# Attention and gated MLP on one core: two more steps of score tiles, six more changes of V's bank, joins of maxima moved by a step, and an uneven split of the last output tile

## The chip, the core and the metric

The kernel runs on one core of one Trainium2 chip. The metric is the device time of one execution in microseconds (us). A core has five engines that run side by side, each working through its own instructions in order: TensorE (PE, matmuls; PEld is its weight load), VectorE (DVE), ScalarE (ACT), GpSimd (POOL) and SyncE (SP), which here only issues DMAs. They wait for each other through semaphores. An engine whose next instruction waits does nothing else in the meantime, and that holds for the DMAs that an engine issues too.

## What is computed

The reference, cut to what matters (S = 2048 rows, D = 512, 32 heads of 16, MLP width 1376):

```python
def _A_ref(x, wqkv, wo):
    qkv = ...                                  # x @ wqkv, split into heads
    scores = jnp.einsum("bhqd,bhkd->bhqk", q, k) * (Dh ** -0.5)
    p = _softmax(scores, axis=-1)
    o = jnp.einsum("bhqk,bhkd->bhqd", p, v)
    return o.transpose(...).reshape(B, S, D) @ wo
def _B_ref(x, w1, b1, w2, b2):
    return gelu(x @ w1 + b1) @ w2 + b2
xn = _layernorm(x)
out = x + _A_ref(xn, wqkv, wo) * _silu(_B_ref(xn, w1, b1, w2, b2))
```

## The kernel before

The first part (to about 437 us) does the layer norm, the projections and the MLP, whose result goes to DRAM (`g_d`). All of the change lies in the second part, the attention with the output projection.

**Units and steps.** Heads are taken in 8 groups of 4, queries in 4 chunks of 512: 32 *units* (`u`) of 16 *steps* each, steps `n` = 0 to 512. A step handles 128 keys of one unit. Every step writes four tiles of transposed scores (*T*, `t_one`, L760, banks `ps`, `two`, `pst` of the matmul memory), which ScalarE turns into exponentials (L763, L765), and it multiplies the exponentials of the step before by the values (*V*, `pv_step`, L832), into one bank for each unit. After step 16 of a unit, VectorE copies that bank out (L839).

**Maxima.** The exponentials need the row maxima of the scores beforehand. So the scores are computed once more, not transposed, one to two units ahead (*S*, `s_op`, L212), and VectorE reduces each tile to maxima (L218), two heads by two halves at a time. 588 of the 2048 tiles are done in the first part; `due(n)` says how many are to be done by step n: three a step, and two in the second step of the units 1 to `FEW`. The scores end at step `DONE` - 1 = 492. When a unit has all its maxima, VectorE *joins* them (`s_end0`, L274), transposes them (`s_turn`, L263), POOL splits them in two (L265, L266: tile `mh`), and after two to three more V the maxima are *sent* to DRAM (`s_send`, L296). From there SP loads them as two more rows of the query tile `qt` (`load_mh`, L182), which the first T of the unit needs. For the last unit, 31, two of the four writes of the maxima are issued by POOL.

**Banks.** S uses a ring of banks, in turn. In the units 1 to `FEW` = 16, V takes another bank than in the unit before (lines in `pv_step`: V's old bank goes into the ring, a bank of the ring becomes V's). From unit 17 on V keeps its bank, so the first V of a unit waits until VectorE has copied the unit before out of it; the first step of these units has another order (`FIRST`).

**Order within a step.** `manual_schedule` keeps the instructions in the order of the code. A string gives it: T, S, X and Y (two halves of a score tile), V, and from `DONE` on *H* and W. The entries of `todo[n, i]` come behind the T tile with number i of step n; pos=3 is behind the fourth.

**Output.** From `DONE` on there are no scores. H (`w_halves`) is a twelfth to an eighth part of two output tiles: 6 matmuls, in pairs, on the halves of the rows; the operands `oh`, `ol` are made two steps earlier by ScalarE (L938) and POOL (L941) in `w_two`. A pair of the 10 first output tiles takes 8 H in four steps. `gate` (ScalarE tanh L894, VectorE L895) prepares the gate of each token tile, `w_gate` (L966) multiplies the projection by it, `w_add` (L971) adds x, and a DMA (L972) writes it. V is done for two steps at once in every second step. The last output tile (t = 15) is split in two halves of 256 columns.

**Other work in these steps.** The sums of exponentials are inverted (`o_den`, L859 RECIPROCAL) in step 16u + 25, that is in the step with `ka` = 9 of the next unit; POOL divides by them (`o_div`, L871) in step 16u + 31.

Of the kernel before, what the change touches and what calls it, by code (L numbers as in the profile page):

```python
# [16 lines left out]
P = 128  # L17
S = 2048
D = 512
H = 32  # L20
DH = 16
KT = D // P
NT = S // P
# [11 lines left out]
NW = 10  # L35
EARLY = 4
AHEAD = ((-3, 0), (-3, 3), (-2, 0), (-2, 3))
DONE = 493
FILL0 = 2
APART = 5  # L40
HB = 5
# [2 lines left out]
ORDER = {0: "TTTTV", 2: "TSTTSTV", 3: "XTSTTYSTV"}  # L44
FIRST = "STXTTSYTV"
TWO = ("HTTTTHWV", "TTTTHHV")
BOTH = {DONE: "HHTTTTV", DONE + 3: "HHTTTTWV"}
SOON = 588
FEW = 16
SIDES = ((1, 1), (0, 0), (0, 1), (1, 0))  # L50
HC = CH // 2
PAIRED = 26
KB = 3
VP = (((0, 8),), ((0, 2), (1, 2)), ((2, 3),))
VB = (((0, 2), (1, 2)), ((1, 8),))
XB = 6
BANKS = ("ttvt", "xtmt", "ttvt")


@with_exitstack  # L60
def fused(ctx: ExitStack, tc: tile.TileContext, x, wqk, wv, wo, w1, b1, w2, out):
    nc = tc.nc
# [32 lines left out]
    def zip2(cols):  # L95
        return cols.rearrange("p (a b) -> p b a", a=2)

    def unzip(cols):
        return cols.rearrange("p (b a) -> p a b", a=2)

    def halves(cols):
        return cols.rearrange("p (a b) -> p a b", a=2)
# [12 lines left out]
    NU = NG * NCH  # L115
# [71 lines left out]
    later, ended, errands, sent = [], [], [], set()  # L187

    def units_of(u):
        return (u,) if u >= PAIRED else (u - u % 2, u - u % 2 + 1)  # L190

    def tick():
        for e in later:
            e[0] -= 1

    def flush():
        while later and later[0][0] <= 0:
            u = later.pop(0)[1]
            s_send(u)
# [36 lines left out]
    def s_op(op):  # L236
        if op == "S":
            if whole:
                s_whole(whole.pop(), 1)
            else:  # L240
                whole.append(jobs.pop(0))
                s_whole(whole[0], 0)
        elif op == "X":
            if not cut:
                cut[:] = [jobs.pop(0), 0]
            ps, pool = s_tile(True)
            x = s_mm(ps, cut[0], 0, 0, cut[1] * HC, HC)
            cut[2:] = [ps, pool, x]
        else:
            job, n, ps, pool, x = cut  # L250
            hold = nc.tensor.nop().ins
            tc.add_manual_dep(hold, x.name, SYNC, reason="row tile done")
            s_mm(ps, job, 1, HC, n * HC, HC)
            s_max(ps, job, slice(0, 2), n)
            s_ring.append(pool)
            cut[1] += 1
            if n:
                cut.clear()

    def s_turn(u, nm):  # L260
        later.append([8 if u == NU - 1 else 12, u])
        nt = qring.tile([P, 2 * GH * NCH], F32, name="nt", bufs=1)
        nc.vector.transpose(nt, nm)  # L263
        mh = MH[u] = qring.tile([P, 2, 2 * GH * NCH], F32R, name="mh", bufs=1)
        nc.gpsimd.tensor_copy(mh[:, 0], nt)  # L265
        nc.gpsimd.tensor_sub(mh[:, 1], nt, mh[:, 0].bitcast(F32))  # L266

    def s_end0(u):
        ended.remove(u)
        us = units_of(u)  # L270
        w = u % 2 * GH * NCH
        nm = nms[u // 2 % 2]
        mx = MX.pop(u).rearrange("p a b c n -> p (a b) (c n)")
        nc.vector.tensor_reduce(nm[:, w:w + GH * NCH], mx, axis=AX.X, op=OP.max, negate=True)  # L274
        if u == us[-1]:
            if "seen" in prog or u == NU - 1:
                s_turn(us[0], nm)
            else:
                put_off.append((us[0], nm))
        del QS[u]  # L280
        if "seen" in prog:
            ask_qs(u + 2)
        else:
            load_qs(u + 2)
# [127 lines left out]
    with ExitStack() as s1:  # L412
# [13 lines left out]
        def load_x(t, eng=nc.sync):  # L426
            xs[t] = w1k.tile([P, D], F32, name="xt", bufs=XB)
            eng.dma_start(xs[t], x[t * P:(t + 1) * P, :])
# [20 lines left out]
        def norm(t):  # L449
            xns[t] = w1k.tile([P, D], F32, name="xn", bufs=4)  # L450
            nc.vector.tensor_scalar(xns[t], xs.pop(t), mv[:, t, 0:1], ve[:, 4, t:t + 1],
                                    op0=OP.subtract, op1=OP.mult)
            if t + XB < NT:
                load_x(t + XB)

# [50 lines left out]
        for k in range(KT):  # L506
            nc.sync.dma_start(wv_r[:, k], wv[:, k])
        for t in range(6, XB):
            load_x(t)
# [209 lines left out]
    def quad(n, at):  # L719
        us = first[n]  # L720
        for u, b in zip(us, BANKS[n]) if at == 0 else ():
            if b == "t":
# [99 lines left out]
    def pv_step(u, k):  # L822
        g = u // NCH
        if k == 0:
            if 0 < u <= FEW:
                s_ring.insert(1, v_home.pop())
# [88 lines left out]
        w_round([(t, k) for t in T3], ot[NCH - 1][:, k].rearrange("p (t s) -> p t s", s=P), lo)  # L915

    def cols(t):
        n = 2 if t == NT - 1 else 1
        return [slice(i * D // n, (i + 1) * D // n) for i in range(n)]

    def w_mul(t, ks, parts=(0, 1)):
        if t not in PW:
# [41 lines left out]
    def w_gate(t, i=0):  # L964
        gx, cs = GX[t], cols(t)[i]
        nc.vector.scalar_tensor_tensor(gx[:, 0, cs], PW[t][i][:, :cs.stop - cs.start], 0.5, gx[:, 0, cs],  # L966
                                       op0=OP.mult, op1=OP.mult)

    def w_add(t, eng, i=0):
        gx, cs = GX[t], cols(t)[i]  # L970
        eng.tensor_add(gx[:, 0, cs], gx[:, 0, cs], gx[:, 1, cs])  # L971
        (nc.gpsimd if t < NW else nc.sync).dma_start(out[t * P:(t + 1) * P, cs], gx[:, 0, cs])  # L972

    def w_out(t, eng):
        w_gate(t)
# [2 lines left out]
    todo = {}  # L978

    def at(n, f, *a, pos=3):  # L980
        todo.setdefault((n, pos), []).append((f, a))
# [4 lines left out]
    def due(n):  # L986
        return min(4 * L, SOON + 3 * n - min(FEW, max(0, n - 1) // 16))

    for u in range(NU):
        g, c = divmod(u, NCH)  # L990
        if c == 0 and g == KB:
            for i in range(6):
                at(52 + i // 2, load_k, g, (i,), nc.gpsimd, 0, CH)
                at(56 + i // 2, load_k, g, (i,), nc.gpsimd, CH, CH)
                at(64 + i // 2, load_k, g, (i,), nc.gpsimd, S // 2, S // 2)
        elif c == 0 and g > KB:
            for i in range(6):
                at(64 * (g - KB + 1) + 6 + i, load_k, g, (i,), nc.gpsimd)
        if u >= 2:
            at(16 * u - 14, load_qt, u)  # L1000
            last = units_of(u)[-1]
            need = min(n for n in range(L) if due(n) >= 64 * (last + 1))
            need += 10 if u < PAIRED else 6 if u < NU - 1 else 2
            at(max(16 * u - 14, need), load_mh, u)
        if u < NU - 1:
            at(16 * u + 17, o_move, u, pos=0)
            at(16 * u + (25 if u < NU - 2 else 19), o_den, u, pos=0)
            at(16 * u + (27 if u < NU - 2 else 20), o_dn, u)
            at(16 * u + (31 if u < NU - 2 else 23), o_div, u, nc.gpsimd)
    T3 = range(NT - NCH, NT)  # L1010
    late = range(NW, NT)
    for t in range(NW):
        n = DONE + 4 * (t // 2)
        at(n - 3 + t % 2, load_gx, t)
        if t % 2 == 0:
            for i in range(2):
                at(n + i - 2 if t else n + 2 * i - 7, w_two, t, 2 * i)
            for i in range(4):
                for j in range(2):
                    at(n + i, w_halves, t, i % 2 * 2 + j, i // 2, pos="H")  # L1020
        at(n + t % 2, gate, t)
        at(n + 3, w_out, t, nc.gpsimd, pos="W")
    for i, t in enumerate(late):
        n = L - 2 * len(late) - 1 + 2 * i
# [10 lines left out]
    for n in range(L + 1):  # L1035
        ua, ka = divmod(n, 16)
        want = due(n) - due(n - 1)
        i = 0
        if put_off and ka > 1:
            s_turn(*put_off.pop(0))  # L1040
        else:
            for u in list(ended):
                if u >= PAIRED or ka > 2 and since.setdefault(u, n) < n:
                    s_end0(u)
        order = BOTH.get(n, TWO[n % 2]) if n >= DONE else ORDER[want] if n else ORDER[0]
        if want == 3 and ka == 0 and ua > FEW:
            order = FIRST
        for op in order:
            if op in "SXY":
                s_op(op)  # L1050
            elif op == "H":
                f, args = todo[n, "H"].pop(0)
                f(*args)
            elif op == "W":
                for f, args in todo.get((n, "W"), []):
                    f(*args)
            elif op == "V":
                for v in range(n - 1, n) if n < DONE else range(n - 2, n) if n % 2 == 0 else ():
                    if v >= 0:
                        pv_step(*divmod(v, 16))  # L1060
                for _ in range(4):
                    tick()
                flush()
            else:
                if EARLY <= 4 * n + i < 4 * L:
                    t_one(ua, ka, i, True)
                for f, args in todo.get((n, i), []):
                    f(*args)
                i += 1
# [17 lines left out]
    for t, i in [(t, i) for t in T3 for i in range(len(cols(t)))]:  # L1087
        w_mul(t, KS if t == NT - 1 else KS[2:] if t == T3[2] else KS[3:], (i,))
        w_gate(t, i)
        w_add(t, nc.vector, i)  # L1090


# [35 lines left out]
```

## Time and profile before

| | before |
|---|---|
| median of 3 runs | 1495.87 us (1495.28 to 1495.96) |
| the profiled execution | 1496.0 us |
| its span, first to last instruction | 1494.2 us |
| granted TensorE clock over the span | 0.999 |
| VectorE, maxima in bank `ps` (L218) | 1658 x 687 ns |
| ScalarE, exponentials of 1024 columns (L765) | 511 x 1019 ns |
| V (L832), two banks' names together | 4096 matmuls of 598 ns, four at a time |

How to read it: the span is that of one profiled execution, and what lies between it and the execution's time (1.8 us) is around the instructions. Durations of neighbours on one engine overlap, since an instruction starts before the one ahead of it is through: two maxima of 0.68 us take 1.29 us together. A row of the timeline gives the start from the span's begin, the time until the last of the merged instructions ended, engine, line, operation, tiles, and in brackets the idle time before it and what ended it. Steps are found in the timeline by V: V of the second part comes once a step until the scores end, then twice in every second step.

### The profile page before, as it was taken

The page shows a single profiled execution, that of the slowest core. Times are in us where ns is not written, and L with a number is a line of the kernel's source. Part 1 is how long each engine was busy: PE and PEld are TensorE (multiplying, and loading weights), DVE is VectorE, ACT ScalarE, POOL GpSimd, SP SyncE. Part 2 cuts the span into 40 slices and gives each one's busy share as a digit, 9 for nine tenths or more (in the row PEclk, how much of TensorE's full clock was granted, in tenths as well). Part 3 has the DMA queues.
Part 4 walks back from the last instruction along what each step waited for, and adds up shares of the span by engine and source line. Part 5 has one row for each costly group of instructions (what it writes and reads, how often), then busy time and mean ns, then how long its engine had stood idle before and what let it go on. Part 6 is the DMA issues. An engine that isn't in the chain of part 4 may idle for free.

```text
span 1494.2 us, 31296 instructions
## 1 busy us (share of the span) xinstructions
PE 1487.4 (100%) x12234; PEld 870.5 (58%) x12234; DVE 1396.7 (93%) x2292; ACT 1202.8 (81%) x1884; POOL 358.9 (24%) x378
## 2 busy tenths in 40 slices
PE   9999999999999999999999999999999999999998
PEld 8899999999974444444444444444444444444456
DVE  8799999999999999999999999999999999999935
ACT  4333433434359999999999999999999999999994
POOL 4246666657540021011100200100010000000154
PEclk9999999999999999999999999999999999999999
DMA  6526354474341122114210511411141111110163
GB/s 212 160 74 175 105 158 128 147 167 139 118 126 27 34 51 42 41 49 68 53 30 22 86 31 34 73 31 33 34 70 31 35 31 34 42 31 20 51 209 118
DMA packets 78275, 116.57 MB, mean 78 GB/s; under 512 B 28180, under 2 KB 28436, under 8 KB 76952
## 3 DMA queue, kind: packets, MB, share of 16 engines
q1 hardware_dynamic: 73632, 99.27, 24.3%
q0 software_dynamic: 4144, 14.72, 5.1%
q8 instruction: 96, 1.57, 0.5%
q10 hardware_dynamic: 352, 0.59, 0.1%
q14 instruction: 51, 0.42, 0.1%
HBM read 84.09 MB, written 25.97 MB: 74 GB/s over the span
## 4 chain that ended last, share of the span: by engine, by line
PE 99%; DVE 1%; DMA 0%; ACT 0%; issue 0%; ACTq 0%
PE ps L832 27%; PE ps L212 19%; PE ps L623 10%; PE pst L760 8%; PE two L760 7%; PE pv L832 6%; PE ps L760 4%; PE sp L623 4%; PE pv L212 4%; PE pst L623 2%; PE pv L623 2%; PE ps L960 1%; PE pst L494 1%; PE ps L494 1%; PE pv L960 1%; PE pv L474 0%
## 5 line engine op out<-in xcount | busy, mean ns | idle before, releaser
L218 DVE TENSOR_REDUCE mx<-ps 128x2 f32<-128x512 f32 x1658 | 1077.1, 687 | 43.0 <-PE ps L212 17.1
L765 ACT ACTIVATE slot<-two 128x1024 f32<-128x1024 f32 x511 | 520.6, 1019 | 0.0
L832 PE MATMUL ps<-slot,vsb 128*17 128x512 f32 (+1 forms) x3328 | 436.3, 598 | 0.0
L763 ACT ACTIVATE slot<-ps 128x512 f32<-128x512 f32 x515 | 307.6, 597 | 13.6 <-PE ps L760 6.9
L763 ACT ACTIVATE slot<-pst 128x512 f32<-128x512 f32 x511 | 309.5, 606 | 0.0
L212 PE MATMUL ps<-kt,slot 48*128 48x256 f32 (+1 forms) x980 | 299.0, 361 | 0.0
L212 PEld LDWEIGHTS ps<-kt,slot 48*128 48x128 f32 x980 | 164.5, 184 | 219.6 <-DVE mx L218 211.2
L218 DVE TENSOR_REDUCE mx<-pv 128x2 f32<-128x512 f32 x390 | 266.6, 684 | 8.1 <-PE pv L212 1.0
L623 PE MATMUL ps<-slot,w1h 64*128 64x512 f32 x1088 | 201.6, 376 | 0.0
L212 PE MATMUL ps<-kt,qz 48*128 48x512 f32 x512 | 194.1, 379 | 0.0
L760 PE MATMUL two<-qt,kt 50*128 50x512 f32 x766 | 188.7, 379 | 0.4 <-ACT slot L765 0.4
L760 PE MATMUL ps<-qt,kt 50*128 50x512 f32 x387 | 184.3, 476 | 0.0
L760 PE MATMUL pst<-qt,kt 50*128 50x512 f32 x383 | 161.4, 422 | 0.0
L623 PEld LDWEIGHTS ps<-slot,w1h 64*128 64x128 f32 x1088 | 141.3, 186 | 13.0
L623 PE MATMUL ps<-slot,w1l 64*128 64x512 f32 x544 | 138.9, 376 | 0.0
L212 PE MATMUL pv<-kt,slot 48*128 48x256 f32 (+1 forms) x378 | 137.8, 365 | 0.0
L212 PE MATMUL ps<-slot,slot 48*128 48x256 f32 (+1 forms) x458 | 137.4, 361 | 0.0
L212 PEld LDWEIGHTS ps<-slot,slot 48*128 48x128 f32 x458 | 76.2, 184 | 95.7 <-DVE mx L218 92.1
L395 POOL TENSOR_TENSOR hl<-hg,hh 128x512 fp32r<-128x512 f32 x76 | 95.9, 1281 | 142.1 <-ACT hh L394 126.2
L377 ACT ACTIVATE hg<-ps,b_sb 128x512 f32<-128x512 f32 x44 | 27.9, 684 | 125.2 <-PE ps L623 117.9
L832 PEld LDWEIGHTS ps<-slot,vsb 128*17 128x17 f32 (+1 forms) x3328 | 56.8, 96 | 99.8 <-issue 96.1
L212 PEld LDWEIGHTS pv<-kt,slot 48*128 48x128 f32 x378 | 69.5, 184 | 77.5 <-DVE mx L218 74.6
(214 smaller groups left out, 2329.3 us busy)
## 6 DMA issues: line engine op xcount, KB each, us to landing
raw<-in_w SPq DMA_DIRECT2D x88, 256.0 KB
qk_h<-hh SPq DMA_DIRECT2D x32, 256.0 KB
qk_l<-hl SPq DMA_DIRECT2D x32, 256.0 KB
qt<-qk_h SPq DMA_DIRECT2D x128, 64.0 KB
slot<-qk_h SPq DMA_DIRECT2D x92, 64.0 KB
g_d<-hg POOLq DMA_DIRECT2D x16, 256.0 KB, 4.0
qt<-qk_l SPq DMA_DIRECT2D x64, 64.0 KB
dn<-den_d SPq DMA_DIRECT2D x32, 128.0 KB
```

The lines of the kernel that those rows point to most:

```text
L212: return nc.tensor.matmul(ps[:, c0:c0 + w], QS[u][r, p, qi * P:(qi + 1) * P], zip2(kts[u // NCH % KB][p][r, k0:k0 + w]), start=True, stop= ...
L218: nc.vector.tensor_reduce(MX[u][:, 2 * p:2 * p + 2, qi, ki][:, heads, parts], ps.rearrange("p (n c) -> p n c", c=HC), axis=AX.X, op=OP.max)
L377: nc.scalar.activation(halves(raw), unzip(ph.pop(u)), AF.Gelu_apprx_tanh, bias=b1_sb[:, u[2]:u[2] + 1])
L395: nc.gpsimd.tensor_sub(hl, raw, hh.bitcast(F32))
L494: nc.tensor.matmul(ps, w, cols, start=n == s == k == 0, stop=n == 2 and k == KT - 1)
L623: i = nc.tensor.matmul(ps, lhs[r], rhs[r], start=first, stop=last).ins
L760: nc.tensor.matmul(ps, kts[g % KB][p][r, k * P:(k + 1) * P], zip2(QT[u][r, p, :]), start=True, stop=True)
L763: nc.scalar.activation(PT[u, k][:, 2 * p + a, :], ps, AF.Exp, scale=SCALE)
L765: nc.scalar.activation(PT[u, k][:, :2], TP["two"], AF.Exp, scale=SCALE)
L832: nc.tensor.matmul(PV[u][32 * j:32 * j + w, :], vsb.rearrange("p t w -> p (t w)")[:, k * H * VW + h:k * H * VW + h + w], PT[u, k][:, j, :] ...
L960: HALF[0] = nc.tensor.matmul(PW[i][0], OTS[i, k][x][r], zip2((wo_h, wo_l)[y][r, k]), start=k == 0 and side == 0 and n == 0, stop=k == KT - ...
```

## The change

Four parts:

1. `FEW` goes from 16 to 22, `DONE` from 493 to 495. Six more units (17 to 22) change V's bank, have two score tiles in their second step, and do not use `FIRST`. The six tiles are done in steps 493 and 494, with the usual order of a step with scores. The H of the first pair of output tiles, which stood in steps 493 to 496, are now all in steps 495 and 496, four each. All else of the output (`load_gx`, `w_two`, `gate`, `w_out`) stays at its step.
2. The maxima of unit 31 are complete in step 494 instead of 492; its load moves to a place of its own, `M`, in step 496 behind V and ahead of T. The load of units 26 to 29 comes one step later relative to its scores; unit 30's maxima are sent one V earlier.
3. A join does not start in a step with `ka` = 9.
4. The last output tile is split at column 352 instead of 256. Its first part is added by POOL and written from SP, its second part is added by VectorE and written from ScalarE's queue.

```diff
-DONE = 493
+DONE = 495
...
-BOTH = {DONE: "HHTTTTV", DONE + 3: "HHTTTTWV"}
+BOTH = {DONE: "HHTTTTHHV", DONE + 1: "HHHHVMTTTTW", DONE + 2: "HHTTTTV", DONE + 3: "HHTTTTWV"}
 SOON = 588
-FEW = 16
+FEW = 22
...
+LAST = 352
...
     def s_turn(u, nm):
-        later.append([8 if u == NU - 1 else 12, u])
+        later.append([8 if u >= NU - 2 else 12, u])
...
     def cols(t):
-        n = 2 if t == NT - 1 else 1
-        return [slice(i * D // n, (i + 1) * D // n) for i in range(n)]
+        return [slice(0, LAST), slice(LAST, D)] if t == NT - 1 else [slice(0, D)]
...
-        (nc.gpsimd if t < NW else nc.sync).dma_start(out[t * P:(t + 1) * P, cs], gx[:, 0, cs])
+        (nc.gpsimd if t < NW else nc.scalar if i else nc.sync).dma_start(out[t * P:(t + 1) * P, cs], gx[:, 0, cs])
...
-            need += 10 if u < PAIRED else 6 if u < NU - 1 else 2
-            at(max(16 * u - 14, need), load_mh, u)
+            need += 10 if u < PAIRED else 7 if u < NU - 2 else 6 if u < NU - 1 else 2
+            at(max(16 * u - 14, need), load_mh, u, pos=3 if u < NU - 1 else "M")
...
     for t in range(NW):
-        n = DONE + 4 * (t // 2)
+        n = DONE - 2 + 4 * (t // 2)
...
-                    at(n + i, w_halves, t, i % 2 * 2 + j, i // 2, pos="H")
+                    at(n + i if t else DONE + i // 2, w_halves, t, i % 2 * 2 + j, i // 2, pos="H")
...
             for u in list(ended):
+                if ka == 9 and u < NU - 2:
+                    continue
                 if u >= PAIRED or ka > 2 and since.setdefault(u, n) < n:
                     s_end0(u)
...
-            elif op == "W":
-                for f, args in todo.get((n, "W"), []):
+            elif op in "WM":
+                for f, args in todo.get((n, op), []):
                     f(*args)
...
-        w_add(t, nc.vector, i)
+        w_add(t, nc.gpsimd if t == NT - 1 and i == 0 else nc.vector, i)
```

The order of POOL's instructions around unit 31's maxima (`mh`), first before, then after the change. `slot_6896` with `dn` is the division of unit 29, `ol` the operand of H made in steps 495 and 496; line numbers after the change are one higher up to L896.

```order
L265 CAST mh<-nt 128x32
L266 TENSOR_TENSOR mh<-nt,mh 128x32
L296 DMA mh_d<-mh 16x2x32 x2
L871 TENSOR_TENSOR slot_6896<-slot_6896,dn 64x512
L941 TENSOR_TENSOR ol<-slot_6895,oh 128x512 x2
```

```order
L266 CAST mh<-nt 128x32
L267 TENSOR_TENSOR mh<-nt,mh 128x32
L872 TENSOR_TENSOR slot_6896<-slot_6896,dn 64x512
L941 TENSOR_TENSOR ol<-slot_6895,oh 128x512
L297 DMA mh_d<-mh 16x2x32 x2
L941 TENSOR_TENSOR ol<-slot_6895,oh 128x512
```

The two DMA writes have moved behind the division and the first `ol`.

VectorE's order at the end of the scores, before and after; L895 (L896 after) is the gate of token tiles 0 and 1, L966 the first two output tiles' evacuation, L839 the copy of V of unit 30.

```order
L218 TENSOR_REDUCE mx<-ps 128x2 x2
L218 TENSOR_REDUCE mx<-pv 128x2
L274 TENSOR_REDUCE nm_597<-mx 128x16
L263 STREAM_TRANSPOSE nt<-nm_597 128x32
L895 SCALAR_TENSOR_TENSOR gx<-slot_20192,gx 128x512 x2
L966 SCALAR_TENSOR_TENSOR gx<-ps,gx 128x512 x2
L839 COPY os<-ps 128x512
```

```order
L896 SCALAR_TENSOR_TENSOR gx<-slot_20153,gx 128x512
L219 TENSOR_REDUCE mx<-ps 128x2 x2
L219 TENSOR_REDUCE mx<-pv 128x2
L275 TENSOR_REDUCE nm_597<-mx 128x16
L264 STREAM_TRANSPOSE nt<-nm_597 128x32
L896 SCALAR_TENSOR_TENSOR gx<-slot_20153,gx 128x512
L840 COPY os<-ps 128x512
L966 SCALAR_TENSOR_TENSOR gx<-ps,gx 128x512 x2
```

The first gate stands ahead of the last three maxima now, and the copy of V's bank ahead of the two evacuations.

TensorE's order around the first T of unit 31 (step 496; `qt_6899` is its query tile), before and after. The rows named `vsb` are V of steps 494 and 495.

```order
L760 MATMUL ps<-qt_6899,kt_112 128x512
L760 MATMUL two<-qt_6899,kt_112 128x512 x2
L760 MATMUL pst<-qt_6899,kt_112 128x512
L832 MATMUL ps<-slot_20205,vsb 17x512 x4
L832 MATMUL ps<-slot_20236,vsb 17x512 x4
```

```order
L833 MATMUL ps<-slot_20162,vsb 17x512 x4
L833 MATMUL ps<-slot_20210,vsb 17x512 x4
L761 MATMUL ps<-qt_6899,kt_112 128x512
L761 MATMUL two<-qt_6899,kt_112 128x512 x2
L761 MATMUL pst<-qt_6899,kt_112 128x512
```

V has moved ahead of T, so T is the last of step 496, and the H of step 497 follow it.

## The prediction

> **What bounds the kernel now.** I read the page first. Its lines of the span, of TensorE and of the chain that ended last:
>
> ```profile
> span 1494.2 us, 31296 instructions
> ...
> PE 1487.4 (100%) x12234; PEld 870.5 (58%) x12234; DVE 1396.7 (93%) x2292; ACT 1202.8 (81%) x1884; POOL 358.9 (24%) x378
> ...
> PE 99%; DVE 1%; DMA 0%; ACT 0%; issue 0%; ACTq 0%
> ```
>
> TensorE is busy all through and the chain hardly leaves it, so a term counts only where it makes TensorE issue later. A shorter wait elsewhere is worth nothing. Next, the table of stretches, which I asked for with borders that follow the program: units 1 to 15 (240 steps), the 96 steps in which V of units 17 to 22 begins, three places of two steps each, the stretch from the V of step 492 to the V of step 498, and the end after the last matmul. The columns are length, busy time of each engine, granted clock, DMA share and rate.
>
> ```profile
> 469.21:946.12 476.91, 476.91 (x3811) 209.95 (x3810) 454.33 (x753) 475.12 (x721) 50.22 (x77) 1.00 0.22 45
> 973.92:1166.28 192.36, 192.36 (x1539) 84.61 (x1537) 185.36 (x309) 190.08 (x289) 10.53 (x16) 1.00 0.19 41
> 864.56:868.60 4.04, 4.04 (x35) 1.75 (x34) 4.04 (x9) 4.02 (x8) 0.00 (x0) 1.00 0.18 41
> 1248.61:1252.72 4.11, 4.11 (x34) 1.81 (x32) 4.11 (x10) 4.09 (x8) 0.21 (x1) 1.00 0.33 88
> 1376.99:1381.02 4.03, 4.03 (x35) 1.75 (x33) 4.03 (x10) 4.01 (x8) 0.21 (x1) 1.00 0.02 2
> 1417.02:1433.93 16.91, 16.47 (x138) 9.84 (x136) 5.93 (x11) 14.52 (x25) 6.79 (x9) 1.00 0.32 103
> 1491.00:1492.00 1.00, 0.00 (x0) 0.00 (x0) 0.34 (x1) 0.00 (x0) 0.00 (x0) 1.00 0.71 248
> 1492.00:1493.00 1.00, 0.00 (x0) 0.00 (x0) 0.00 (x0) 0.00 (x0) 0.00 (x0) 0.70 0.39 131
> ```
>
> A step with scores takes 476.91/240 = 1.987 us while ScalarE (475.12 of 476.91) and VectorE (454.33) are nearly full too. Any extra VectorE work in such a step can hold up a bank that TensorE wants.
>
> **Term 1, banks of units 17 to 22.** In these units V keeps its bank, waits until the copy of the unit before has read it, and the step's maxima queue behind that copy. The 96 steps took 192.36; at the rate of units 1 to 15, which change banks, they would take 96 x 1.987 = 190.76. The change brings them to that form: **-1.6 us**. Their six moved score tiles (one less in a unit's second step) save no time by themselves, as those steps do not get shorter than 1.987 in units 1 to 15 either. Bounds: 0 if it is the place in the program and not the bank, -1.8 if none of the small stalls of this stretch returns.
>
> **Term 2, joins.** VectorE's timeline in the last of the three places, and the group row of the copy that term 1 speaks of:
>
> ```profile
> 1378.38 0.28 DVE L274 TENSOR_REDUCE nm<-mx 128x16 f32<-128x128 f32 x1
> 1378.57 0.24 DVE L859 RECIPROCAL dr<-dr 128x16 f32<-128x16 f32 x1
> ```
>
> ```profile
> L839 DVE COPY os<-ps 128x512 f32<-128x512 f32 x25 | 17.0, 682 | 1.0 <-PE ps L832 1.0
> ```
>
> A join and a reciprocal, 0.28 and 0.24 long, stand in one step there: the stretches of 4.04, 4.11 and 4.03 against 3.97 for two steps, 0.27 together. Moved to other steps, a join may still cost a little: **-0.2 us**, between -0.3 and +0.1.
>
> **Term 3, steps 493 to 498.** Here most is moved. The rows are the timeline of before around the old end of the scores (start, duration, engine, line, tiles, count, idle time before); the second fence has the first T of unit 31 and the rows around it, the last two what DMAs took.
>
> ```profile
> 1416.61 1.29 DVE L218 TENSOR_REDUCE mx<-ps 128x2 f32<-128x512 f32 x2
> ...
> 1417.02 1.05 PE L832 MATMUL ps<-slot,vsb 128*17 128x512 f32 x8
> 1417.82 0.68 DVE L218 TENSOR_REDUCE mx<-pv 128x2 f32<-128x512 f32 x1
> 1417.90 0.60 ACT L763 ACTIVATE slot<-pst 128x512 f32<-128x512 f32 x1
> 1418.00 0.48 PE L960 MATMUL ps<-wo_h,oh 64*128 64x512 f32 x2
> ...
> 1419.40 0.38 PE L760 MATMUL ps<-qt,kt 50*128 50x512 f32 x1
> ...
> 1419.49 0.25 POOL L266 TENSOR_TENSOR mh<-nt,mh 128x32 fp32r<-128x32 f32 x1
> ...
> 1419.82 0.60 ACT L763 ACTIVATE slot<-ps 128x512 f32<-128x512 f32 x1 [1.32 <-PE ps L760]
> ...
> 1420.03 1.06 POOL L296 DMA_DIRECT2D mh_d<-mh  x2 [0.29 <-POOL mh L266]
> ...
> 1421.16 1.27 POOL L871 TENSOR_TENSOR slot<-slot,dn 64x512 f32<-64x512 f32 x1
> 1421.22 0.60 ACT L763 ACTIVATE slot<-pst 128x512 f32<-128x512 f32 x1
> ...
> 1421.69 0.64 ACT L894 ACTIVATE slot<-gx 128x512 f32<-128x512 f32 x1
> ...
> 1422.23 0.53 SPq L182 DMA_DIRECT2D qt<-mh_d  x2
> 1422.37 0.69 DVE L895 SCALAR_TENSOR_TENSOR gx<-slot,gx 128x512 f32<-128x512 f32 x1 [3.23 <-ACT slot L894]
> ...
> 1422.93 1.91 PE L832 MATMUL ps<-slot,vsb 128*17 128x512 f32 x16
> ```
>
> ```profile
> 1427.17 0.64 ACT L938 ACTIVATE oh<-slot 128x512 fp32r<-128x512 f32 x1
> ...
> 1427.91 0.38 PE L760 MATMUL ps<-qt,kt 50*128 50x512 f32 x1
> ...
> 1427.95 1.28 POOL L941 TENSOR_TENSOR ol<-slot,oh 128x512 fp32r<-128x512 f32 x1 [5.52 <-ACT oh L938]
> ```
>
> ```profile
> DMA to landing us min/median/max: 1.6/1.7/1.7
> ```
>
> ```profile
> q1 hardware_dynamic: 12, 0.02, 4.5%
> ```
>
> The first of them is that of the two writes of unit 31's maxima on POOL; the second is queue q1 between 1422.23 and 1423.76: the 16 KB that SP's two loads of them (L182) move are all there within 1.53 us of the issue. T of unit 31 came at 1427.91, so before the change this chain was done four microseconds early.
>
> Now the same steps after. Let 0 be the start of V in step 494, the new last step with scores; it is 2 x 1.987 = 3.97 after the V at 1417.02.
> 1. VectorE. The gate of token tile 0 (L895) stays in step 493, but the three maxima of step 494 now stand behind it. Step 493's V starts at -1.99, its last exponential 0.88 later (1417.90 - 1417.02), the tanh 0.47 after that (1421.69 - 1421.22): -0.64 to 0.00. The gate starts at +0.04, and a further operation 0.60 after its forerunner (1.29 for two, less 0.69): maxima at 0.64, 1.24, 1.84, the last ending at 2.52.
> 2. TensorE. The first H tiles need the banks of the first two maxima. Before, H started 0.98 after V and found the second freed at 0.88. Now the second is free at 1.24 + 0.68 = 1.92: H waits **0.95**. No row shows this case; it costs 0 if the gate finds VectorE early, 0.95 by the order of rows, and I take 0.95.
> 3. T of step 495 comes 1.40 after H starts (1419.40 - 1418.00): 3.35. ScalarE's last exponential follows at +1.82 and oh at +2.29 (1421.69 - 1419.40): 5.64 to 6.28.
> 4. POOL. The two DMA writes of maxima stood right behind mh; now the division (1.27) and ol (1.28) are ahead of them, and ol needs oh: 6.28 + 0.14 to 7.70. The DMAs take 1.06 for two, the second starts at 8.23 and lands 1.7 later, at 9.9; SP's loads then need 1.53: **T of step 496 at 11.5**.
> 5. TensorE meanwhile: T 0.43, six H of 0.65 (two take 1.40 with some 0.1 of start), two V in 1.85: free at 9.6. It waits **1.9**, and everything behind T in TensorE's queue waits too.
> 6. From there three T with only two H between each pair, and H of step 498 needs oh and ol of step 496, which are ready 2.93 and 4.35 after T (2.29 + 0.64, then 0.14 + 1.28). Three matmul pairs of it 0.65, T 0.43, and small starts: V of step 498 at 11.5 + 5.7 = 17.2.
>
> So this V comes 3.97 + 17.2 = 21.2 after 1417.02 instead of 16.91: **+4.3 us**. If nothing waited, TensorE's own work in between would be 3.97 + 0.98 + 12 x 0.65 + 4 x 0.43 + 1.85 + some 0.3 of starts = 16.6, that is -0.3; if the load takes longer by half a microsecond, +5. I take 4.3, as each link has its row. From that V on both programs have the same two-step pattern, which TensorE fills, so nothing is won back. The tanhs in steps 493 and 494 cost ScalarE 0.5 each, hidden: before T of step 495 it idled 1.32 in the row at 1419.82. SP's loads of gx now stand ahead of the writes of maxima, but they wait for nothing, so they are issued long before.
>
> **Term 4, the last tile.** The first and the last of 24 narrow matmuls, VectorE's last rows, and POOL's group of adds:
>
> ```profile
> 1487.42 0.27 PE L107 MATMUL ps<-wo_h,oh 128*128 128x256 f32 x1
> ...
> 1489.99 0.28 PE L107 MATMUL two<-wo_h,slot 128*128 128x256 f32 x1
> ```
>
> ```profile
> 1489.67 0.42 DVE L966 SCALAR_TENSOR_TENSOR slot<-ps,slot 128x256 f32<-128x256 f32 x1
> ...
> 1490.91 0.42 DVE L971 TENSOR_TENSOR slot<-slot 128x256 f32<-128x256 f32 x1
> ```
>
> ```profile
> L971 POOL TENSOR_TENSOR gx<-gx 128x512 f32<-128x512 f32 x8 | 10.2, 1281 | 0.1
> ```
>
> The first part's gate, 352 columns, takes 0.42 + 0.27 x 96/256 = 0.52 (512 columns took 0.69) and ends at 1490.19. POOL's add of 352, scaled from 1.28 for 512 (the group row), is 0.88: 1491.1 to 1491.2. The second part of 160: gate and add of 0.32 each after the last matmul at 1490.27 end at 1490.95, on ScalarE's queue. The later of them is 0.15 ahead of the 1491.33 of before, less some for the larger transfer: **-0.1 us**, between -0.3 and +0.2. The matmuls are 0.112 apart; I take 160 columns as proportional, 0.07, though no row shows them. [...]
>
> **Sum.** -1.6 - 0.2 + 4.3 - 0.1 = +2.4. The profiled execution took 1496.0 (span 1494.2 and 1.8 around it), so 1498.4; it lies 0.13 above the median of the three runs, 1495.87, so **1498.3**. A measurement of this kernel can tell about 0.2% (3.0 us) from no change, and 2.4 is inside that.
>
> **The rivals.**
> - *POOL's order does not decide.* If the maxima arrive by 9.6, T of step 496 follows V at once. Then VectorE's copy of V's bank (0.68, and the next 0.60 after its start) and the gating of the first output tile behind it (0.69, as other 512-column ones) free H's second bank at about 10.95, and V of step 498 comes at 15.4: +2.5 instead of +4.3, 1496.5. For it: SP's half of the writes is early. Against it: POOL works in order.
> - *All is hidden*: term 3 is -0.3, total 1493.7. Against it: two of the waits follow from instructions that stand in one queue.
> - *The clock falls* while TensorE waits, and the kernel becomes slower. The last matmul ended at 1490.27, and in the stretch 1492.00 to 1493.00 the granted clock is 0.70 on average, so it fell about 2.1 us after. The forecast wait is 1.9; from about 2.1 on this rival decides. Then the 3.9 us of T and H behind it would take up to twice as long, part of it under ol's wait: +3, 1501.3. [...]
> - *The change does not do what it says*: units 17 to 22 stay at 2.004 a step, since VectorE lags there for another cause. Term 1 is 0: 1499.9.
>
> **How the numbers follow.** Forecast 0.52 (its own range 1497.3 to 1499.3), POOL's order 0.17, hidden 0.11, clock 0.12, no gain of banks 0.08. The range leaves out hidden and most of clock: 1495.4 to 1500.2. Slower by over 0.2% is above 1498.86: 0.3 of the forecast, clock and no gain, 0.36. Faster is below 1492.9: a quarter of hidden, 0.03. Same: 0.61.
>
> **What would show it.** Right: the 96 steps near 190.8; a wait of TensorE ahead of the first H of step 495 on VectorE; POOL's DMAs of maxima behind ol; T of step 496 some 1.9 after V's end, and the stretch from the V of step 492 to that of 498 near 21.2. Wrong: T right behind V, or a clock under 1.00 in this stretch.

## The result, and the profile after

The changed kernel takes **1503.53 us** (median of 5 runs, 1503.30 to 1504.01) against 1495.96 for the kernel before (5 runs, 1495.28 to 1496.53): a ratio of **1.0051**, 95% interval 1.0038 to 1.0065. It is slower by 7.6 us. The forecast was 1498.3, with a range of 1495.4 to 1500.2: the measured time lies 3.3 us above the range.

The page of the changed kernel, with the lines that answer to those of before:

```profile
span 1501.6 us, 31294 instructions
...
PE 1489.4 (99%) x12230; PEld 873.7 (58%) x12230; DVE 1396.6 (93%) x2291; ACT 1202.9 (80%) x1884; POOL 359.8 (24%) x379
...
PE 97%; DVE 1%; DMA 1%; ACT 0%; issue 0%; POOL 0%; ACTq 0%; SPq 0%; POOLq 0%
```

The span grew by 7.4, TensorE's busy time by only 2.0, and TensorE's share of the chain fell from 99% to 97%. So most of the loss is time in which TensorE stood still. The table of stretches of the changed kernel, by the same borders of the program: units 1 to 15, the 96 steps of units 17 to 22, the V of step 492 to the V of step 498, from there to the V of step 512; then from the start of the last matmul to the last byte of output, and the rest of the span. Columns as before: length, busy time of PE, PEld, DVE, ACT and POOL, granted clock, DMA share and rate.

```profile
469.18:946.05 476.87, 476.87 (x3812) 210.13 (x3811) 454.52 (x753) 475.26 (x722) 50.22 (x77) 1.00 0.22 45
977.81:1168.61 190.80, 190.80 (x1527) 84.01 (x1526) 181.76 (x302) 189.94 (x289) 11.58 (x16) 1.00 0.19 40
1415.14:1436.90 21.76, 19.44 (x146) 12.39 (x144) 8.85 (x17) 14.01 (x24) 6.93 (x9) 0.92 0.33 107
1436.90:1475.00 38.10, 38.10 (x336) 23.05 (x334) 19.32 (x21) 37.78 (x63) 23.53 (x23) 1.00 0.61 198
1493.51:1496.09 2.58, 0.28 (x3) 0.12 (x2) 0.65 (x2) 0.00 (x0) 0.80 (x1) 1.00 0.56 203
1496.09:1501.56 5.47, 0.00 (x0) 0.00 (x0) 0.00 (x0) 0.00 (x0) 0.00 (x0) 0.56 0.00 0
```

The borders give the account of the 7.4 us:

| From | to | before | after | difference |
|---|---|---|---|---|
| start | V of step 492 | 1417.02 | 1415.14 | -1.88 |
| V of step 492 | V of step 498 | 16.91 | 21.76 | +4.85 |
| V of step 498 | first matmul of the last tile | 53.49 | 53.64 | +0.15 |
| that | start of the last matmul | 2.57 | 2.97 | +0.40 |
| that | last byte of output | 2.73 | 2.58 | -0.15 |
| that | end of the span | 1.46 | 5.47 | +4.01 |

The first two rows are what the forecast spoke of, -1.8 and +4.3. The last is one that it did not have: for 5.47 us nothing runs that the busy columns count. The timeline of the end, and the rows of the program's last line (its waits and drains, with count, shortest, median and longest in ns, first and last start):

```profile
1493.38 0.93 POOL L971 TENSOR_TENSOR slot<-slot 128x352 f32<-128x352 f32 x1 [9.03 <-DVE slot L966]
...
1494.18 0.32 DVE L971 TENSOR_TENSOR slot<-slot 128x160 f32<-128x160 f32 x1
1494.33 0.33 SPq L972 DMA_DIRECT2D out<-slot  x1
1494.54 0.36 ACTq L972 DMA_DIRECT2D out<-slot  x1
```

```profile
L1126 POOLq DRAIN  x3: 46/102/7425, 1493.3 to 1501.3; - x3
L1126 SPq DRAIN  x3: 7/7/13, 1496.7 to 1501.0; - x3
```

POOL's first drain starts at 1493.3 and takes 7.43: it ends at 1500.8, 6.5 after POOL's add (1493.38 + 0.93 = 1494.31). SP reached its own drain at 1496.7, when all output was there; then the end waited 4.1 for POOL (to 1500.8), and all engines' last drains start at 1501.0 or later. The kernel before has the same drain, in the same view:

```profile
L1124 POOLq DRAIN  x3: 46/102/7983, 1479.9 to 1493.9; - x3
```

There POOL's last instruction ran from 1479.90 to 1481.38. The drain ended at 1487.9, also 6.5 later, while TensorE still had work until 1490.27. It cost nothing, and no chain or wait of that profile named it.

The stretch from the V of step 494 to the V of step 498, in the timeline of the changed kernel:

```profile
1419.11 1.05 PE L833 MATMUL ps<-slot,vsb 128*17 128x512 f32 x8
1419.19 0.69 DVE L896 SCALAR_TENSOR_TENSOR gx<-slot,gx 128x512 f32<-128x512 f32 x1 [0.55 <-ACT slot L895]
1419.80 1.28 DVE L219 TENSOR_REDUCE mx<-ps 128x2 f32<-128x512 f32 x2
...
1420.63 0.99 PE L960 MATMUL ps<-wo_h,oh 64*128 64x512 f32 x2 [0.47 <-DVE mx L219]
...
1423.33 0.79 SPq L297 DMA_DIRECT2D mh_d<-mh  x2
1423.38 1.28 POOL L872 TENSOR_TENSOR slot<-slot,dn 64x512 f32<-64x512 f32 x1
...
1425.61 1.28 POOL L941 TENSOR_TENSOR ol<-slot,oh 128x512 fp32r<-128x512 f32 x1 [0.95 <-ACT oh L938]
...
1426.83 1.06 POOL L297 DMA_DIRECT2D mh_d<-mh  x2
...
1427.27 1.91 PE L833 MATMUL ps<-slot,vsb 128*17 128x512 f32 x16
...
1429.02 0.53 SPq L183 DMA_DIRECT2D qt<-mh_d  x2
...
1430.93 0.45 PE L761 MATMUL ps<-qt,kt 50*128 50x512 f32 x1 [1.74 <-DMA qt<-mh_d]
...
1435.39 0.18 PEld L960 LDWEIGHTS pv<-wo_h,ol 64*128 64x128 f32 x1 [0.18 <-POOL ol L941]
```

Step by step it is the forecast chain: the gate (L896) ahead of step 494's maxima, POOL's two DMA writes behind the division and ol, SP's loads behind their landing, and T of step 496 after a wait of 1.74.

### The profile page after: what moved, and what is told of

Read it like the earlier page. It is cut to its first block, busy times and chain, and to the rows that moved or that the text cites. A ratio compares the mean times of both kernels' runs of the same rounds, so it can differ in the third digit from the quotient of the medians.

```text
span 1501.6 us, 31294 instructions
## 1 busy us (share of the span) xinstructions
PE 1489.4 (99%) x12230; PEld 873.7 (58%) x12230; DVE 1396.6 (93%) x2291; ACT 1202.9 (80%) x1884; POOL 359.8 (24%) x379
## 4 chain that ended last, share of the span: by engine, by line
PE 97%; DVE 1%; DMA 1%; ACT 0%; issue 0%; POOL 0%; ACTq 0%; SPq 0%; POOLq 0%
PE ps L833 25%; PE ps L213 19%; PE ps L624 10%; PE pv L833 8%; PE pst L761 8%; PE two L761 7%; PE ps L761 4%; PE sp L624 4%; PE pv L213 3%; PE pst L624 2%; PE pv L624 2%; PE ps L960 1%; PE pst L495 1%; PE ps L495 1%; PE pv L960 1%; PE pv L475 0%
## 5 line engine op out<-in xcount | busy, mean ns | idle before, releaser
L219 DVE TENSOR_REDUCE mx<-ps 128x2 f32<-128x512 f32 x1690 | 1095.5, 687 | 46.5 <-PE ps L213 17.9
L833 PE MATMUL ps<-slot,vsb 128*17 128x512 f32 (+1 forms) x3072 | 402.8, 598 | 0.0
L213 PE MATMUL ps<-kt,slot 48*128 48x256 f32 (+1 forms) x1002 | 302.1, 360 | 0.0
L213 PEld LDWEIGHTS ps<-kt,slot 48*128 48x128 f32 x1002 | 167.9, 184 | 223.1 <-DVE mx L219 215.3
L219 DVE TENSOR_REDUCE mx<-pv 128x2 f32<-128x512 f32 x358 | 245.0, 684 | 6.0 <-PE pv L213 0.4
L213 PE MATMUL ps<-slot,slot 48*128 48x512 f32 (+1 forms) x480 | 140.9, 360 | 0.0
L213 PEld LDWEIGHTS ps<-slot,slot 48*128 48x128 f32 x480 | 79.3, 184 | 101.2 <-DVE mx L219 97.7
L833 PE MATMUL pv<-slot,vsb 128*17 128x512 f32 (+1 forms) x1024 | 134.8, 598 | 0.0
L213 PE MATMUL pv<-kt,slot 48*128 48x256 f32 (+1 forms) x354 | 129.5, 366 | 0.0
L761 PEld LDWEIGHTS two<-qt,kt 50*128 50x128 f32 x766 | 106.9, 187 | 0.7 <-ACT hg L690 0.4
```

Of the source, the lines that this page charges most:

```text
L213: return nc.tensor.matmul(ps[:, c0:c0 + w], QS[u][r, p, qi * P:(qi + 1) * P], zip2(kts[u // NCH % KB][p][r, k0:k0 + w]), start=True, stop= ...
L219: nc.vector.tensor_reduce(MX[u][:, 2 * p:2 * p + 2, qi, ki][:, heads, parts], ps.rearrange("p (n c) -> p n c", c=HC), axis=AX.X, op=OP.max)
L761: nc.tensor.matmul(ps, kts[g % KB][p][r, k * P:(k + 1) * P], zip2(QT[u][r, p, :]), start=True, stop=True)
L833: nc.tensor.matmul(PV[u][32 * j:32 * j + w, :], vsb.rearrange("p t w -> p (t w)")[:, k * H * VW + h:k * H * VW + h + w], PT[u, k][:, j, :] ...
```

## The experiments

### The end: what POOL's drain costs

Two runs take one part of the new end back each; two put POOL's add into the kernel before.

```diff
# a_add_on_dve: the changed kernel with
-        w_add(t, nc.gpsimd if t == NT - 1 and i == 0 else nc.vector, i)
+        w_add(t, nc.vector, i)
# a_out_on_sp: the changed kernel with
-        (nc.gpsimd if t < NW else nc.scalar if i else nc.sync).dma_start(...)
+        (nc.gpsimd if t < NW else nc.sync).dma_start(...)
# b_add_on_pool: the kernel before with
-        w_add(t, nc.vector, i)
+        w_add(t, nc.gpsimd if t == NT - 1 and i == 0 else nc.vector, i)
# b_add12_on_pool: the kernel before with
-        w_add(t, nc.vector, i)
+        w_add(t, nc.gpsimd if t == T3[0] else nc.vector, i)
```

> The changed kernel with the add of the last tile's 352 columns on VectorE instead of POOL; the split and ScalarE's queue for the second part stay. Theory (POOL's drain): in the changed kernel POOL's last computation ended at 1494.31 and its drain only at 1500.77, 6.46 later; in the kernel before the same drain ended 6.46 after POOL's last row too, but at 1487.85, under other work. With no POOL work near the end the span ends about 1.5 after the last output byte, at some 1497.9 instead of 1501.6: time about 1499.8. Rival 1 (the second queue, ScalarE's, makes the end late): no change, 1503.5. Rival 2 (the matmuls and the wait in step 496 make up all of the loss): no change either.

> The changed kernel with the DMA of the last 160 columns on SP's queue as before; POOL's add of 352 columns stays. POOL's drain: no change, 1503.5 within 0.5, the drain's end still 6.46 after POOL's add. Rival (ScalarE's queue makes the end late): about 1499.5.

> The kernel before with one thing changed: the add of the first 256 columns of the last tile on POOL. POOL's drain: the gate ends at 1490.08, an add of 256 columns takes some 0.72, 6.46 of drain and 0.8 from the drain's end to the span's end follow: span 1498.1 instead of 1494.2, time about 1499.9. Rival (no drain to speak of): the add is 0.3 longer but beside the last matmuls, so 1496.0 within 0.3.

> The kernel before with the add of output tile 12 (the first of the last four) on POOL, so that POOL's last work ends some 3 us earlier than in the run with the last tile's add there. POOL's drain: the gate ends at 1486.37, the add at 1487.7, the drain at 1494.15, the span at 1494.9: 0.7 more than before, 1496.7. Rival (the drain costs only if POOL's row is among the very last rows, or is a fixed surcharge for any late POOL work): 1496.0, or the same +3.9 as with the last tile.

Measured: VectorE's add 1499.42 (ratio to the kernel before 1.0021, 1.0012 to 1.0029), 4.1 less than the change; SP's queue for the last DMA 1503.91 (1.0052, 1.0039 to 1.0065), nothing; POOL's add in the kernel before 1500.14 (1.0026, 1.0016 to 1.0036); tile 12's add there 1497.21 (1.0007, 0.9998 to 1.0016). The times of the kernel before beside these runs had a median of 1496.32. POOL's last row and its drain in the two last runs, first with the last tile's add, then with tile 12's:

```profile
1489.53 0.72 POOL L971 TENSOR_TENSOR slot<-slot 128x256 f32<-128x256 f32 x1 [8.62 <-DVE slot L966]
```

```profile
L1124 POOLq DRAIN  x3: 46/102/7225, 1489.5 to 1497.2; - x3
```

```profile
1487.01 1.28 POOL L971 TENSOR_TENSOR slot<-slot 128x512 f32<-128x512 f32 x1 [5.51 <-DVE slot L966]
```

```profile
L1124 POOLq DRAIN  x3: 46/102/7780, 1487.0 to 1495.3; - x3
```

The drains end at 1496.7 and 1494.8, both 6.5 after the add that stands ahead of them, and the spans end 0.8 later (1497.5 and 1495.5). In the kernel before, the span's end (1494.18) less 0.79 and 6.46 leaves 1486.93 as the last moment at which POOL's work could end for nothing. Tile 12's add ended 1.36 after it and the last tile's 3.33 after it, and by these amounts the spans of the profiled executions grew (1495.54 and 1497.51). So in these runs the drain was neither a fixed surcharge (3.33 of span in one, 1.36 in the other) nor a matter of the queue (1503.91 with SP's, 1503.53 with ScalarE's): each microsecond that POOL worked on past 1486.93, that is 7.25 (6.46 + 0.79) before the end of the kernel before, cost one. (Tile 12's add started 0.6 later than I had reckoned, hence 1497.2 and not 1496.7.) By the medians tile 12's add costs 0.9, and the interval of its ratio reaches down to no change, so that small step rests on the rows of its trace; the last tile's 3.8 are clear. The rival of ScalarE's queue falls.

### The last tile's columns

```diff
# b_split: the kernel before with
-        n = 2 if t == NT - 1 else 1
-        return [slice(i * D // n, (i + 1) * D // n) for i in range(n)]
+        return [slice(0, 352), slice(352, D)] if t == NT - 1 else [slice(0, D)]
```

> The kernel before with only the last tile's split changed, 352 and 160 columns instead of 256 twice (both adds on VectorE, both DMAs on SP). The matmuls of 352 columns are 0.15 apart in the changed kernel, those of 160 0.111, as those of 256 are; twelve of each give 3.13 instead of 2.67, +0.46, while the last gate and add are 0.2 shorter and the last transfer smaller: the span ends 0.0 to 0.3 later, time 1496.0 to 1496.3. If columns alone counted (160 at 0.07), the matmuls would end as before and the span 0.2 to 0.4 earlier.

Measured: 1495.95 (1.0000, 0.9991 to 1.0009). The last matmul starts 0.51 later after the V of step 512, and the last byte lands 0.48 sooner after that matmul. With adds on VectorE and both DMAs on SP the split is worth nothing either way. Two rows of the changed kernel show the distance of the narrow matmuls:

```profile
1493.40 0.28 PE L108 MATMUL two<-wo_l,slot 128*128 128x160 f32 x1
1493.51 0.28 PE L108 MATMUL two<-wo_h,slot 128*128 128x160 f32 x1
```

```profile
1492.03 0.31 PE L108 MATMUL ps<-wo_l,slot 128*128 128x352 f32 x1
1492.18 0.31 PE L108 MATMUL ps<-wo_h,slot 128*128 128x352 f32 x1
```

160 columns are 0.11 apart, as 256 were, and not the proportional 0.07 that the forecast took; 352 are 0.15 apart.

### Steps 493 to 498: who holds up T, and what the clock does

All runs here stand on the run with VectorE's add, whose stretch from the V of step 492 to that of 498 took 21.91 (1414.93 to 1436.84).

```diff
# c_send_on_sp
-            eng = nc.gpsimd if u == NU - 1 and b % 2 else nc.sync
+            eng = nc.sync
# c_one_on_pool
+            eng = nc.gpsimd if u == NU - 1 and b == 3 else nc.sync
# c_busy_wait, in t_one ahead of T's matmul
+        for _ in range(8 if u == NU - 1 and k == i == 0 else 0):
+            nc.tensor.matmul(ps, kts[g % KB][p][r, k * P:(k + 1) * P],
+                             zip2(QT[u - 1][r, p, :]), start=True, stop=True)
# c_gates_later
-        at(n + t % 2, gate, t)
+        at(max(n, DONE) + t % 2, gate, t)
```

> The run with VectorE's add (span 1497.3, time 1499.4) and one more edit: all four DMA writes of unit 31's maxima on SP. POOL's order decides: SP issues all four by some 1425, they land by 1426.7, its loads by 1428.6, before V of step 496 is through (about 1429); TensorE's wait of 1.7 is gone and the clock stays at 1.00; the stretch from the V of step 492 to that of 498 falls from 21.9 to about 19.9 (it can't fall to 16.9, as the H of step 498 still wait for oh and ol, made after step 496's T), time about 1497.4. Rival 1 (SP's own queue is as late, behind its waits): no change. Rival 2 (the fall of the clock cost the bulk): 18.5 or less, 1496 or less.

> The run with VectorE's add and one more edit: only one of the four DMA writes of unit 31's maxima is on POOL, not two. It lands 0.5 earlier (one issue of 0.53 less in front of it), so T of step 496 comes 0.5 earlier and TensorE's wait is about 1.2 instead of 1.75. If any wait of over a microsecond lowers the clock, it falls again some 2.5 after the wait begins, and the stretch is 21.4; if the clock needs a longer wait, it stays at 1.00, and the stretch is 21.4 as well or up to 0.3 less, since oh and ol are what H waits for then. Time 1498.6 to 1498.9.

> The run with VectorE's add and one more edit: ahead of unit 31's first T stand eight matmuls of the unit before's scores into the same bank, about 1.72 in all, whose result is overwritten: TensorE works through the wait for the maxima. The wait itself stays. Theory 1 (the wait is what costs; the fall of the clock is hidden by the wait for ol): the clock stays at 1.00 and the stretch shrinks by only 0.3, to 21.6. Theory 2 (the half clock from 1431.7 to 1435.2 costs its full length, 1.8): the stretch is 20.1 and the time 1497.7.

> The run with VectorE's add and one more edit: the gates of output tiles 0 and 1 stand in steps 495 and 496 instead of 493 and 494. If the gate ahead of step 494's maxima is what holds up the first H, these start about 0.5 earlier after V, the second right behind the first, and all that follows moves with it: stretch 21.4 to 21.0, time 1498.6 to 1498.9. Rival (the maxima themselves, not the gate, are late): no change.

| Run | stretch | TensorE's wait for the maxima | time | ratio (95%) |
|---|---|---|---|---|
| a_add_on_dve | 21.91 | 1.78 | 1499.42 | 1.0021 (1.0012 to 1.0029) |
| c_send_on_sp | 19.97 | none | 1497.60 | 1.0010 (1.0001 to 1.0019) |
| c_one_on_pool | 21.35 | 1.34 | 1498.56 | 1.0017 (1.0008 to 1.0027) |
| c_busy_wait | 21.72 | filled | 1499.45 | 1.0021 (1.0012 to 1.0031) |
| c_gates_later | 25.89 | 2.29 | 1503.71 | 1.0051 (1.0037 to 1.0064) |

With all writes on SP, the loads are issued at 1425.62 and T follows V at once:

```profile
1425.62 0.53 SPq L183 DMA_DIRECT2D qt<-mh_d  x2
...
1426.78 1.91 PE L833 MATMUL ps<-slot,vsb 128*17 128x512 f32 x16
1428.62 0.48 PE L761 MATMUL ps<-qt,kt 50*128 50x512 f32 x1
```

The stretch falls by 1.94, as expected (19.97 for 19.9), and with one write on POOL by 0.56. POOL's order decides when T starts.

**The clock.** It fell in the changed kernel although the wait, 1.74, was shorter than the 2.1 us from which that rival was to decide. Its granted clock, in the table of stretches with three borders put where it changes:

```profile
1428.47:1431.88 3.41, 1.67 (x15) 0.93 (x9) 1.89 (x3) 0.40 (x1) 0.00 (x0) 1.00 0.06 11
1431.88:1435.29 3.41, 3.41 (x18) 3.14 (x16) 0.00 (x0) 3.07 (x6) 1.22 (x1) 0.50 0.42 97
1435.29:1438.70 3.41, 3.41 (x31) 1.52 (x28) 0.69 (x1) 3.41 (x7) 3.09 (x4) 1.00 0.45 169
```

It was 0.50 from 1431.88, 0.95 after T had started again, to 1435.29, for 3.41. Yet the run that kept TensorE at work through the wait, with the clock at 1.00, gained only 0.19 of 21.91, and nothing in the median. Its T was not held up by the added matmuls (3.67 after the V of step 496, and 3.69 without them), and from T to the V of step 498 it took 5.91 instead of 6.08. At full clock TensorE came sooner to the H that reads ol and stood still there:

```profile
1435.98 0.48 PE L963 MATMUL pv<-wo_h,ol 64*128 64x512 f32 x1 [0.65 <-POOL ol L944]
```

At half clock, in the changed kernel, it waited 0.18 for the same operand (the last row of its timeline above), which POOL makes after the T that came late. So of the 3.41 at half clock all but about 0.2 was hidden.

**The gates.** The last run was to gain 0.5 to 0.9 and lost 4.0 in the stretch. Its first half did more than expected: from the V of step 494 to that of step 496 it takes 7.13 instead of 8.17, 1.04 less. But then:

```profile
1430.39 0.45 PE L761 MATMUL ps<-qt,kt 50*128 50x512 f32 x1 [2.29 <-DMA qt<-mh_d]
...
1432.81 0.64 ACT L895 ACTIVATE slot<-gx 128x512 f32<-128x512 f32 x1
...
1433.49 0.69 DVE L896 SCALAR_TENSOR_TENSOR gx<-slot,gx 128x512 f32<-128x512 f32 x1 [4.62 <-DMA ot<-os]
1434.09 1.28 DVE L966 SCALAR_TENSOR_TENSOR gx<-ps,gx 128x512 f32<-128x512 f32 x2
...
1434.83 0.79 PE L960 MATMUL ps<-wo_h,oh 64*128 64x512 f32 x1 [3.32 <-DVE gx L966]
```

I had put the second gate behind unit 31's first exponentials on ScalarE. These wait for the late T, the gate behind them, the output's gating (L966) behind the gate, and H's bank behind that: 3.32. It is a new wait in place of the one taken away, and my expectation had not looked at what stands ahead of the gate on ScalarE.

### Banks, and all in one

```diff
# d_bank_kept: the run with VectorE's add and, in pv_step,
-            if 0 < u <= FEW:
+            if 0 < u <= 16:
# d_send_gates: c_send_on_sp and
-        at(n + t % 2, gate, t)
+        at(DONE if t < 2 else n + t % 2, gate, t)
# d_best: d_send_gates, the last tile as before the change, and
-                at(n + i - 2 if t else n + 2 * i - 7, w_two, t, 2 * i)
+                at(n + i - 2 if t else n + 2 * i - 7, w_two, t, 2 * i, pos="M" if t == 2 and i else 3)
```

> The run with VectorE's add (time 1499.4, 96 steps of units 17 to 22 in 190.80) and one more edit: V changes its bank up to unit 16 only, as before the change, while the score tiles keep their new places (one less in the second step of units 17 to 22). Theory (the bank is what the 1.55 of these steps hang on): V waits for the copy of the unit before again, the 96 steps take 192.4 or a little more, time 1501. Rival (the place of the score tiles alone brought it): 190.8, 1499.4.

> The run with all DMA writes of unit 31's maxima on SP (stretch 19.97, time 1497.6) and one more edit: the gates of output tiles 0 and 1 both stand at the end of step 495, behind step 494's maxima and joins and ahead of unit 31's first exponentials. In the run where they stood in 495 and 496 the V of step 496 came 1.04 earlier after that of step 494 (7.13 instead of 8.17), but the second gate, behind exponentials that wait for unit 31's T, then held up the H of step 497 for 3.3. With both ahead of T only the gain stays: 7.13, stretch 18.9, time 1496.6. Rival (the tanhs delay oh and with it H of step 497): stretch 19.9.

> All that the runs suggest in one kernel: banks and score tiles as in the change; writes of unit 31's maxima on SP; both first gates at the end of step 495; oh and ol for step 498 made ahead of unit 31's first T instead of behind it; last tile as before the change (two halves of 256, add on VectorE, both DMAs on SP). If oh and ol are the last wait of the stretch, it falls from 18.9 to about 17.7 (what TensorE has to do is 16.6 plus a bank's wait of 0.6), the end is that of the kernel before: span 1492.7, time 1494.5, 0.1% faster than before. If another wait takes its place: stretch 18.9, 1495.7.

*The bank kept*: 1500.38 (1.0030, 1.0019 to 1.0041). The 96 steps:

```profile
977.97:1169.63 191.66, 191.09 (x1526) 83.99 (x1526) 181.52 (x301) 189.64 (x288) 11.58 (x16) 1.00 0.19 40
```

Neither theory is right alone. Of 192.36 - 190.80 = 1.56, the bank brings 191.66 - 190.80 = 0.86. The other 0.70 came without it. This run differs from the kernel before not only in the place of the score tiles: `FEW` stays at 22, so units 17 to 22 do not use `FIRST` here either, and the joins have moved. Which of these brings the 0.70, no run tells apart.

*Sends and gates*: the stretch is 18.93 with 7.13 in its middle part, as expected; time 1496.73 (1.0004, 0.9995 to 1.0013), as the kernel before.

*All in one*: 1496.34 (1.0001, 0.9992 to 1.0010), as the kernel before too, and 1.8 above the 1494.5 of the first case. The stretch fell only from 18.93 to 18.70. Its rows (the first is a bank's wait of 0.56 that had been reckoned with):

```profile
1429.71 0.48 PE L960 MATMUL ps<-wo_h,oh 64*128 64x512 f32 x1 [0.56 <-DVE gx L966]
...
1432.02 1.02 ACT L766 ACTIVATE slot<-two 128x1024 f32<-128x1024 f32 x1
...
1432.84 0.38 PE L761 MATMUL ps<-qt,kt 50*128 50x512 f32 x1
1432.92 0.60 ACT L764 ACTIVATE slot<-pst 128x512 f32<-128x512 f32 x1
1433.09 0.48 PE L761 MATMUL two<-qt,kt 50*128 50x512 f32 x2
...
1433.58 0.48 PE L761 MATMUL pst<-qt,kt 50*128 50x512 f32 x1
```

ol is no longer waited for, but TensorE now reaches the T of step 498 so early that its banks are still being read: `two` until 1433.04, then `pst` until 1433.52, and each T starts right behind. ScalarE's exponentials have become the bound of this step.

Of the 5.00 by which the stretch had grown (21.91 against 16.91), the sends bring back 1.94, the gates 1.04 and ol 0.23. The other 1.79 stay (18.70 - 16.91), and the rows above show only a part of where they go. They take back what is gained up to the V of step 492 (1.73 in this run).

## Why the prediction was wrong

**Term 4, the last tile (-0.1 forecast): this step failed.** It read "the later of them is 0.15 ahead of the 1491.33 of before" and ended the kernel with the last DMA. POOL's add near the end also moved POOL's drain, which ended 6.46 after it. The measured term is +4.26 (+0.40 matmuls, -0.15 up to the last byte, +4.01 drain), and four runs show the last part. With VectorE's add the changed kernel took 1499.42, inside the range: the drain alone put the time outside it. It could have been seen beforehand: the rows of the program's last line show a drain of 7.98 us on POOL that began at 1479.9. The prediction didn't use that line, since nothing in the chain of waits led to it. The smaller mistake beside it, 160 columns as proportional, cost 0.4 in the matmuls. In the run with the split alone the shorter tail gave that back; in the changed kernel it gave back 0.15.

**Terms 1 and 2 (-1.6 and -0.2): right in size.** The V of step 492 came 1.88 earlier. For the 96 steps 190.76 were forecast and 190.80 measured. The total holds, since it was read from units 1 to 15, which had the whole new form already. The working gave all of it to the bank, and that is wrong: 0.70 of the 1.56 came without the bank, and whether the moved score tiles "save no time by themselves" stays open. Which part of the remaining 0.3 outside these steps is the joins', no run told apart.

**Term 3 (+4.3): right in mechanism, 0.55 short.** With 0 at the V of step 494, forecast and measured are: TensorE free 9.6 and 10.07, POOL's DMAs 7.70 and 7.72, T 11.5 and 11.82, the wait 1.9 and 1.74, the V of step 498 17.2 and 17.79. The H wait of 0.95 was a good guess: taking the gates out of the way gave 1.04. T came 0.3 later since SP's loads took 1.91 from issue to T, not the 1.53 to the last byte that I used. Behind T the way to the V of step 498 took 5.97 and not 5.7; the half clock is some 0.2 of that difference.

**The rivals.** "POOL's order does not decide" is refuted by the run with SP's writes, and "all is hidden" by the stretch itself (+4.85). "No gain of banks" did not occur. "The clock falls" did occur, under a condition that I had wrong (a wait of 1.74, not of 2.1), and for a price of about 0.2, not 3. So the missing 5 us of the sum (2.4 forecast, 7.4 measured) are 4.0 of drain, 0.55 of term 3 and 0.4 of matmuls.

## What to carry to other kernels

Ask of each engine when its last instruction ends and what it has to do after that: the rows of the program's last line show it, and the chain of waits does not, as long as it is hidden. Here POOL had to be through with its work 7.25 us before the end (6.46 of drain and 0.79 behind it), so short work of the last rows belongs on another engine, even a busier one: VectorE's add took back 4.1. And an instruction that is moved takes the place of its queue with it: POOL's two DMA issues of 1.06 behind ol cost 1.94 of the stretch, and the gate of 0.69 behind exponentials that wait for T held H up for 3.32.

## What the runs showed of the hardware that was not expected

- In seven traces (both kernels, the four runs on the end, the run with the later gates) POOL's drain ended 6.4 to 6.5 us after POOL's last computation, whether that was an add of 0.72 us or an ol of 1.51. In the kernel before and in the changed kernel it was 6.46.
- In two traces the granted clock changed at distances of 3.41 us or a multiple of it. In the changed kernel it was 0.50 for 3.41 (1431.88 to 1435.29), and the next fall, at 1496.73, came 61.44 later, 18 times as long. The 3.41 ahead of the first fall held 1.67 of TensorE's work (49%), those ahead of the second (1493.32 to 1496.73) 0.47 (14%). The run with the later gates shows five such stretches in a row, the third and fourth at 0.50:

```profile
1426.29:1429.70 3.41, 1.82 (x16) 0.27 (x15) 0.69 (x1) 0.00 (x0) 1.02 (x3) 1.00 0.03 7
1429.70:1433.12 3.42, 1.12 (x5) 0.66 (x5) 0.00 (x0) 2.18 (x4) 0.00 (x0) 1.00 0.20 40
1433.12:1436.53 3.41, 1.70 (x8) 1.44 (x10) 1.89 (x3) 0.85 (x2) 2.47 (x2) 0.50 0.52 155
1436.53:1439.94 3.41, 3.41 (x18) 2.71 (x18) 0.00 (x0) 1.72 (x3) 2.43 (x4) 0.50 0.20 77
1439.94:1443.35 3.41, 3.41 (x29) 1.53 (x29) 0.69 (x1) 3.26 (x6) 0.00 (x0) 1.00 0.78 231
```

  Here 1.82 busy of 3.41 (53%) was followed by 1.00, 1.12 (33%) by 0.50, 1.70 (50%) by 0.50 again, and a full stretch by 1.00. In the kernel before, 1.28 (38%, 1488.98 to 1492.39) was followed by 0.50, and in the run with one write of the maxima on POOL 2.08 (61%, 1428.08 to 1431.50) by 1.00. So in these stretches 50% and less stood ahead of half clock, 53% and more ahead of full clock; no run tests whether the busy share is what decides. A wait of 1.74 us came ahead of the fall in the changed kernel, while after the first 1.6 of the 2.29 in the run with the later gates the clock was still 1.00.
- What POOL's drain waits for, no run here can tell.
